# Local attention and a gated MLP on one core: all second chunks of P V get 96 rows, and the keys of each tile lie side by side

## The chip, the cores and the metric

The kernel runs on one core of a Trainium2 chip. The metric is device time in microseconds for one execution, the median of several runs. A core has TensorE (PE in the profile, with its weight loads as PEld), VectorE (DVE), ScalarE (ACT), GpSimd (POOL), SyncE (SP) and 16 DMA engines.

## What is computed

Eight batches, eight heads, 512 local and 32 global tokens, head size 64. Local queries see the keys within 32 positions and all global keys, global queries see everything. The 544 x 8 rows then pass through a two-layer MLP.

```python
s_ll = scale * np.matmul(q_l, k_l.transpose(0, 1, 3, 2))
mask = np.abs(pos[:, None] - pos[None, :]) <= window          # window = 32
s_l = np.concatenate([s_lg, np.where(mask, s_ll, -1e9)], axis=-1)
out_l = np.matmul(sm(s_l), np.concatenate([v_g, v_l], axis=2))
...
h = x @ w_in                       # 4608 x 512 by 512 x 2048
g = h * np.tanh(softplus(h))
return g @ w_out                   # 4608 x 2048 by 2048 x 512
```

## The kernel before

**Attention.** Work goes by batch `b`, head pair `hp` and tile `t` of 128 queries: 128 such units. A tile needs its own 128 keys, 32 on either side where they exist, and the 32 global ones: `WIDTH = [192, 224, 224, 192]` keys. `scores` (L714) makes the scores of two tiles and both heads: per tile and head one float32 matmul for the tile's own 128 keys and one for the remaining 64 or 96. In SBUF (`qk`) the global keys stand in the middle of every tile's 128, so both matmuls read with a stride. A float32 matmul shows in the trace as two passes, each with a weight load of its own, so the eight matmuls of a task leave 16 records. The two heads lie on partitions 0 to 63 and 64 to 127 and run side by side. Then `row_max` (DVE), `expo` (ACT), a split of P into two float16 halves, and a transpose, which a DMA does from batch 1 on, and TensorE in batch 0 (`p_cross`, L774 and L788).

`pv` (L822) makes P V for one tile: for each head three matmuls over the first chunk (the tile's own 128 keys, `vf`) and three over the second (`vc`: neighbours and global keys), 64 columns each. The second chunk has `WIDTH[t] - 128` rows: 64 for tiles 0 and 3, 96 for tiles 1 and 2:

```python
k = WIDTH[t] - 128 if c else 128
for p, vl in ((0, 0), (0, 1), (1, 0)):
    T.matmul(X[u][:, t, h, :], X[pt][:k, ...], X[vx][:k, t, vl, h * 64:(h + 1) * 64], ...)
```

The tiles of `P`, `ph` and `vc` are cleared once at the start; rows 64 to 95 of `vc` are never written for tiles 0 and 3 and stay zero. The global queries have tasks of their own (`g_scores` L860, `g_pv` L914).

**MLP.** It runs over 17 blocks of 256 tokens, in float16 halves. Blocks 0 to 5 take M1 (L958), Mish on ACT, a split into `G` on ACT and DVE, and M2 (L1200). Later blocks replace M1 by a Strassen-like scheme (L1127). M2 follows M1 by `LAG2` slots, a slot being one attention unit. The weights come as 8-byte floats. DVE rebuilds each of 32 loads of 512 KB by three bit operations (L517, L524, L526), TensorE sums squares for a scale (`ws`, L538), and the scaled weights are split with the help of TensorE (L580).

**Order.** A planner (`Plan`) gives each task a cost, a priority (its slot) and buffers, and writes the order of each engine at build time; a few numbers (`BLK2`, `LAGX`, `BOOST`, `CONV1`, ...) set the slots. On the chip each engine and each DMA queue works off its list in that order.

Of the kernel before, what the change touches and what calls it, by code (L numbers as in the profile page):

```python
# [10 lines left out]
F32 = mybir.dt.float32  # L11
# [12 lines left out]
B, H, SL, SG, D = 8, 8, 512, 32, 64  # L24
HP = H // 2
# [2 lines left out]
NF = 8  # L28
TB = 256
NBLK = B * 2 + 1  # L30
KW = 640
SCALE = 0.125
EPS = 1e-9
PSC = 4096.0
# [5 lines left out]


WIDTH = [192, 224, 224, 192]
GC = 64

ST0 = 6
GLATE = 4
# [2 lines left out]
PE, DVE, ACT, POOL, DMA = "PE", "DVE", "ACT", "POOL", "DMA"  # L49
# [253 lines left out]
def attn_mish_kernel(ctx: ExitStack, tc: tile.TileContext, qk, vm, vg, qg, w1, w2, consts_in, out, w64):  # L303
    nc = tc.nc
    V, A, T, G = nc.vector, nc.scalar, nc.tensor, nc.gpsimd
# [25 lines left out]

    rings(sb,

          ("vraw", 1, [128, HP, 4, 128], F32), ("vgraw", 2, [128, 2, 128], F32), ("qg", 2, [128, HP, 64], F32),
          ("vgf", 2, [128, 2, 2, 128], F16),

          ("nm", 6, [128, 1], F32), ("sums", 3, [128, 4, 2], F32), ("rs", 2, [128, 4, 2], F32),
# [222 lines left out]
    parted = set()  # L560
# [6 lines left out]

    def w_split(j):

        parted.add(j)  # L570
        w = j // 8
        f, c, k = W[:, j + j // 8 + 1, :], sw[:, w:w + 1], ("W", j + j // 8 + 1)
        hi, lo, d = [wslot(j), "hi"], [wslot(j), "lo"], ("dg", w)
        pl.add([(ACT, act(1024)), (DVE, dve2(1024))], 0, lambda e: scaled(e, wh(j, 0), f, c), r=[k, ["sw", w]], w=[wslot(j)])
        if j in BY_PE:
            for hf in range(2):
                rest, cols = ("rest", j, hf), slice(hf * 512, (hf + 1) * 512)

# [60 lines left out]
               r=[sv, rg], w=[g])  # L639

    def qk_load(b, hp):
        stream(DMA, dma(576), lambda: load(X["qk", b, hp], qk[b, hp]), 4608, new=[("qk", ("qk", b, hp))])

    def loc(k, j, n):

        a = k[:, SL + 160 * j:SL + 160 * j + 64]
        return bass.AP(a.tensor, a.offset, [list(a.ap[0]), [160, n], [96, 2], list(a.ap[-1])])

    def v_hi(b, hp):
        vf = ("vf", b, hp)  # L650
# [45 lines left out]
    def scores(b, hp, t):  # L696
        qk, s = ("qk", b, hp), [("s", b, hp, t // 2, h) for h in range(2)]

        def go():
            for u in (t, t + 1):  # L700
                a0, c0, k = SL + 160 * u, cols(u).start, qk
                for rest in range(2):
                    for h in range(2):
                        r = slice(h * 64, h * 64 + 64)
                        if rest:
                            n = (WIDTH[u] - 128) // 32
                            x = X[k][r, a0 - 32 if u else SL + 64:][:, :32]
                            x = bass.AP(x.tensor, x.offset, [list(x.ap[0]), [96, n], list(x.ap[-1])])
                            o = X[s[h]][:, c0 + 128:c0 + WIDTH[u]]
                        else:  # L710
                            x = X[k][r, a0:a0 + 64]
                            x = bass.AP(x.tensor, x.offset, [list(x.ap[0]), [96, 2], list(x.ap[-1])])
                            o = X[s[h]][:, c0:c0 + 128]
                        T.matmul(o, X[k][r, u * 128:(u + 1) * 128], x, start=True, stop=True)  # L714
        pl.add(PE, 920, go, r=[qk], new=[("sc", s[0]), ("sc", s[1])])

    def cols(t):

        a = WIDTH[t - 1] if t % 2 else 0
        return slice(a, a + WIDTH[t])  # L720
# [42 lines left out]
    def p_cross(b, hp, t):  # L763

        P, pt, PT = ("P", b, hp, t), ("pt", b, hp, t), ("PT", b, hp, t)

        edge = WIDTH[t] - 128

        def go():
            for c in range(2):  # L770
                rows = edge if c else 128
                for h in range(2):
                    a = h * 224 + c * 128
                    T.matmul(X[PT][:rows, (c * 2 + h) * 128:(c * 2 + h + 1) * 128], X[P][:, a:a + rows], ident, is_transpose=True,  # L774
                             start=(h == c == 0), stop=False, skip_group_check=True)
        pl.add(PE, 430, go, r=[P, "consts"], new=[("h", PT)], rows=0)

        def part(p, c, rows):
            return X[pt][:rows, p * 4 + c * 2:p * 4 + c * 2 + 2, :].rearrange("p n q -> p (n q)")

        def each(fn, w=512):
            for c in range(2):
                rows = edge if c else 128
# [28 lines left out]
    def pv(b, hp, t):  # L812
        pt, vf, vc, (g, ts) = ("pt", b, hp, t), ("vf", b, hp), ("vc", b, hp), group(b, hp, t)
        u, first = ("U", *g), t == ts[0]

        def go():
            for h in range(2):
                n = 0
                for c, vx in ((0, vf), (1, vc)):
                    k = WIDTH[t] - 128 if c else 128  # L820
                    for p, vl in ((0, 0), (0, 1), (1, 0)):
                        T.matmul(X[u][:, t, h, :], X[pt][:k, p * 4 + (c * 2 + h if b < TURNED else h * 2 + c), :],  # L822
                                 X[vx][:k, t, vl, h * 64:(h + 1) * 64], start=(n == 0), stop=(n == 5))
                        n += 1
        pl.add(PE, 360, go, r=[pt, vf, vc], w=() if first else [u], new=[("u", u)] if first else ())
# [27 lines left out]
    def g_scores(b, hp):  # L853
        q, k, g = ("qg", b), ("qk", b, hp), ("g", b, hp)

        def go():
            for c0, n in ((16, 256), (0, 16)):
                for half in range(2):
                    rhs = loc(X[k], 2 * half, 2) if c0 else X[k][:, SL + GC + 16 * half:SL + GC + 16 * half + 16]
# [64 lines left out]
    def blk_x(blk):  # L924
        return (("xh", blk // 2), ("xl", blk // 2), blk % 2 * TB) if blk < 2 * B else (("xh", "g"), ("xl", "g"), 0)

    def blk_parts(blk):
        return [[x, (hp, blk % 2)] for x in blk_x(blk)[:2] for hp in range(HP)]

    def blk_start(blk):  # L930
        c = ("c", blk)
# [299 lines left out]
    BLK2 = 33.028  # L1231
    BLK3 = 39.967
    LAGX = 19.134
    BLOCKS = [9, 17, max(25, int(BLK2)), max(33, int(BLK3))]
    PACE = 0.790
    MORE = 3.680
    S1 = [int(BLOCKS[s // NF] + PACE * (s % NF)) if s < 4 * NF else s + max(18, int(LAGX)) + (int(MORE) if s >= ST0 * NF else 0) for s in range(len(steps))]
    assert all(a <= z - (n % NF == NF - 1) for n, (a, z) in enumerate(zip(S1, S1[1:])))
    LAG2 = 4
    LATER = 18  # L1240
    BOOST = 84.202
    BOOST2 = -31.868
# [6 lines left out]

    splits = []  # L1250
    F0 = 50.843
    FSTEP = 0.607
# [140 lines left out]
    RATE1 = 0.062
    CONV2 = 2.335
    RATE2 = 0.514
    FIRST1 = 6.564
# [26 lines left out]
    for i, x in enumerate(ORDER.split()):  # L1423
        a, n = x[0], int(x[1:] or 0)
# [82 lines left out]
```

## Time and profile before

| | |
|---|---|
| time, median of 3 runs | 961.41 us (961.21 to 962.45) |
| profiled execution, its own time | 960.51 us |
| its span, first to last instruction | 958.7 us |
| mean granted TensorE clock, share of full | 0.990 |
| PE busy | 927.6 us |
| DVE busy, ACT busy | 659.1 us, 575.4 us |

The profiled execution lies 0.9 us below the median. Its time exceeds its span by 1.8 us.

### The profile page before, as it was taken

Reading aid. Unit: us, or ns where it says so; the run is one execution under the profiler, and the core shown is the slowest. Engines: PE = TensorE matmul, PEld = TensorE weight load, DVE = VectorE, ACT = ScalarE, POOL = GpSimd, SP = SyncE. Lnnn points to the kernel's source line nnn. Section 1 sums busy time; section 2 is a strip of 40 time slices with the busy share of each in tenths; the row PEclk is TensorE's granted clock in tenths of the full one; section 3 lists DMA queues with packets and bytes.
Section 4 is the critical chain, followed back from the end, with each engine's and each line's share of the span. In section 5 each row is a group of like instructions: output and inputs, shape, how many; then the busy total and the mean of one; then the engine's idle time right before and its main releaser. Section 6 shows DMA issues by size and latency. Waiting matters only on the chain.

```text
span 958.7 us, 25031 instructions
## 1 busy us (share of the span) xinstructions
PE 927.6 (97%) x10180; PEld 662.5 (69%) x10180; DVE 659.1 (69%) x1869; ACT 575.4 (60%) x1292; POOL 31.3 (3%) x56
## 2 busy tenths in 40 slices
PE   3879999999999999999999999999999999999997
PEld 2647667768776676777777777777777777677673
DVE  6998747757869998798668855786578554843231
ACT  3566867758767687677667665766566553322230
POOL 6120000000000000000000000000000000000000
PEclk9989999999999999999999999999999999999999
DMA  9973125767845756745545654565445440000000
GB/s 355 344 224 130 26 61 128 138 151 121 188 82 104 146 139 114 144 114 93 109 98 125 129 115 103 118 143 108 98 108 89 78 73 26 19 23 1 23 23 23
DMA packets 203683, 106.26 MB, mean 111 GB/s; under 512 B 179632, under 2 KB 189872, under 8 KB 202544
## 3 DMA queue, kind: packets, MB, share of 16 engines
q1 hardware_dynamic: 198816, 87.62, 43.1%
q0 software_dynamic: 3888, 14.16, 4.2%
q10 hardware_dynamic: 864, 2.88, 0.8%
q8 instruction: 80, 1.31, 0.6%
q14 instruction: 35, 0.29, 0.1%
HBM read 46.42 MB, written 8.91 MB: 58 GB/s over the span
## 4 chain that ended last, share of the span: by engine, by line
PE 93%; DMA 2%; DVE 2%; ACT 1%; POOL 1%; issue 0%; SPq 0%; DVEq 0%; ACTq 0%; POOLq 0%
PE o L1200 37%; PE h L1127 22%; PE h L958 13%; PE U L822 7%; PE s L714 7%; PE g L860 2%; PE gu L914 2%; PE rest L580 2%; DMA raw<-in_w 1%; DMA W<-in_w 1%; PE ws L538 1%; DMA gpt<-gph 1%; DVE W L524 1%; DVE W L526 1%; PE PT L774 1%; POOL vc L353 0%
## 5 line engine op out<-in xcount | busy, mean ns | idle before, releaser
L1200 PE MATMUL o<-W,G 128*128 128x512 f16 x1632 | 379.2, 379 | 0.0
L1200 PEld LDWEIGHTS <-G 128*128 128x128 f16 x1632 | 151.8, 98 | 156.9 <-issue 0.3
L1127 PEld LDWEIGHTS <-W 128*128 128x128 f16 x2640 | 152.4, 98 | 13.3
L737 ACT ACTIVATE P<-P,nm 128x192 f32<-128x192 f32 (+1 forms) x256 | 117.5, 460 | 37.6 <-DVE nm L728 34.9
L958 PE MATMUL h<-xh,W 128*128 128x256 f16 x768 | 138.6, 273 | 0.5 <-ACT EE L1004 0.5
L958 PEld LDWEIGHTS <-W 128*128 128x128 f16 x1152 | 108.6, 98 | 18.8 <-issue 1.7
L958 PE MATMUL h<-xl,W 128*128 128x256 f16 x384 | 104.6, 272 | 0.0
L728 DVE CUSTOM_DVE_ANT_0 P<-s,consts 128x192 f32<-128x192 f32 (+1 forms) x256 | 90.0, 368 | 16.2 <-PE s L714 10.1
L1127 PE MATMUL h<-xh,W 128*128 128x128 f16 x960 | 88.1, 219 | 0.0
L822 PEld LDWEIGHTS <-pt 128*128 128x128 f16 (+2 forms) x1536 | 69.0, 97 | 25.1 <-ACT pt L428 1.1
L1127 PE MATMUL h<-xl,W 128*128 128x128 f16 x480 | 82.8, 219 | 0.0
L754 DVE SCALAR_TENSOR_TENSOR ph<-P,ph 128x384 f16<-128x384 f32 (+1 forms) x112 | 63.9, 588 | 21.6 <-ACT ph L428 20.2
L714 PEld LDWEIGHTS s<-qk 64*128 64x128 f32 x1024 | 63.4, 190 | 14.9 <-issue 9.9
L714 PE MATMUL s<-qk 64*128 64x128 f32 (+2 forms) x1024 | 73.2, 283 | 0.0
L1127 PE MATMUL h<-raw,W 128*128 128x128 f16 x1056 | 68.1, 219 | 0.0
L421 ACT COPY EE<-h 128x512 f32<-128x512 f32 x44 | 25.8, 586 | 64.4 <-PE h L1127 39.8
L822 PE MATMUL U<-vc,pt 96*128 96x64 f16 (+1 forms) x768 | 60.9, 193 | 0.0
L822 PE MATMUL U<-vf,pt 128*128 128x64 f16 x720 | 57.1, 194 | 1.0 <-ACT pt L428 1.0
L428 ACT ACTIVATE ph<-P 128x384 f16<-128x384 f32 (+1 forms) x108 | 55.9, 539 | 3.5 <-DMA pt<-ph 3.0
L430 DVE TENSOR_SCALAR G<-EE,c 128x512 f16<-128x512 f32 (+1 forms) x59 | 32.7, 555 | 28.5 <-ACT EE L1004 21.1
L872 DVE TENSOR_REDUCE gmx<-g 128x1 f32<-128x272 f32 x32 | 14.1, 441 | 50.6 <-PE g L860 50.5
L428 ACT ACTIVATE ob<-o,c 128x512 f32<-128x512 f32 (+1 forms) x34 | 23.0, 675 | 42.3 <-PE o L1200 42.1
(172 smaller groups left out, 1359.3 us busy)
## 6 DMA issues: line engine op xcount, KB each, us to landing
qk<-in_qk SPq DMA_DIRECT2D x32, 576.0 KB, 4.4
W<-in_w POOLq DMA_DIRECT2D x17, 512.0 KB, 7.7
out<-ob SPq DMA_DIRECT2D x33, 256.0 KB, 2.3
vraw<-in_vm SPq DMA_DIRECT2D x8, 1024.0 KB, 5.7
raw<-in_w POOLq DMA_DIRECT2D x10, 512.0 KB, 5.0
W<-in_w ACTq DMA_DIRECT2D x5, 512.0 KB, 8.3
pt<-ph SPq DMA_TRANSPOSE x112, 3.3
vc<-vgf SPq DMA_DIRECT2D x32, 48.0 KB, 3.1
```

The costliest lines, as they stand in the source:

```text
L421: A.copy(dst, src)
L428: A.activation(out=dst, in_=src, func=AF.Copy, scale=c)
L430: V.tensor_scalar(dst, src, c, None, ALU.mult)
L580: T.matmul(X[rest], X[d], f[:, cols], start=True, stop=False)
L714: T.matmul(o, X[k][r, u * 128:(u + 1) * 128], x, start=True, stop=True)
L728: pl.add(DVE, 77 + 1.03 * w, lambda: V.tensor_tensor_reduce(out=half(P, h, w), in0=X[s][:, cols(t)], in1=mask[:, m0:m0 + w], scale=-SCALE, ...
L737: pl.add(ACT, 460, lambda: A.activation(out=half(P, h, w), in_=half(P, h, w), func=AF.Exp, bias=X[nm], scale=-1.0, accum_out=X[sums][:, t, ...
L754: pl.add(DVE, dve(n), lambda: V.scalar_tensor_tensor(p_part(X[ph], t, 1), p_src(X[P], t), PSC, p_part(X[ph], t, 0), ALU.mult, ALU.subtract ...
L822: T.matmul(X[u][:, t, h, :], X[pt][:k, p * 4 + (c * 2 + h if b < TURNED else h * 2 + c), :], X[vx][:k, t, vl, h * 64:(h + 1) * 64], start= ...
L958: T.matmul(X[h][:, f * TB:(f + 1) * TB], wh(i, wl)[:, off:off + 128], X[x][:, d, o:o + TB], start=(n == 0), stop=(n == 11))
L1127: T.matmul(X[h][:, c:c + 128], form(J + jj, wl)[:, off:off + 128], x(l, d), start=(p in (1, 2, 5) and c == 0 and n == 0), stop=(n == 5), s ...
L1200: T.matmul(X[o], gp(g, blk, i)[:, f, t * 128:(t + 1) * 128], wh(8 + i, wl)[:, f * 512:(f + 1) * 512], start=(turn == 0 and n == 0), stop=( ...
```

## The change

The host lays the keys of each tile side by side: own 128, neighbours and global keys, 832 columns per head pair in place of 640, so one matmul per tile and head makes all its scores. In P V and in the TensorE transposes of batch 0 the second chunk always has 96 rows; for tiles 0 and 3 the last 32 of them meet rows of `vc` that hold zeros. `vgraw` goes from two buffers to one. The planner's numbers differ. The rest of the diff (assertions) issues nothing.

```diff
-KW = 640
+OWN = [0, 192, 416, 640]
+KW = 832
...
-GC = 64
+GC = 128
...
-          ("vraw", 1, [128, HP, 4, 128], F32), ("vgraw", 2, [128, 2, 128], F32), ("qg", 2, [128, HP, 64], F32),
+          ("vraw", 1, [128, HP, 4, 128], F32), ("vgraw", 1, [128, 2, 128], F32), ("qg", 2, [128, HP, 64], F32),
...
-        stream(DMA, dma(576), lambda: load(X["qk", b, hp], qk[b, hp]), 4608, new=[("qk", ("qk", b, hp))])
+        stream(DMA, dma(672), lambda: load(X["qk", b, hp], qk[b, hp]), 5376, new=[("qk", ("qk", b, hp))])
...
-                a0, c0, k = SL + 160 * u, cols(u).start, qk
-                for rest in range(2):
-                    for h in range(2):
-                        r = slice(h * 64, h * 64 + 64)
-                        if rest:
-                            n = (WIDTH[u] - 128) // 32
-                            x = X[k][r, a0 - 32 if u else SL + 64:][:, :32]
-                            x = bass.AP(x.tensor, x.offset, [list(x.ap[0]), [96, n], list(x.ap[-1])])
-                            o = X[s[h]][:, c0 + 128:c0 + WIDTH[u]]
-                        else:
-                            x = X[k][r, a0:a0 + 64]
-                            x = bass.AP(x.tensor, x.offset, [list(x.ap[0]), [96, 2], list(x.ap[-1])])
-                            o = X[s[h]][:, c0:c0 + 128]
-                        T.matmul(o, X[k][r, u * 128:(u + 1) * 128], x, start=True, stop=True)
+                for h in range(2):
+                    r = slice(h * 64, h * 64 + 64)
+                    T.matmul(X[s[h]][:, cols(u)], X[qk][r, u * 128:(u + 1) * 128], X[qk][r, SL + OWN[u]:SL + OWN[u] + WIDTH[u]],
+                             start=True, stop=True)
...
-                rows = edge if c else 128
+                rows = 96 if c else 128
...
-                    k = WIDTH[t] - 128 if c else 128
+                    k = 96 if c else 128
...
-    LAGX = 19.134
+    LAGX = 19.303
...
-    LAG2 = 4
-    LATER = 18
-    BOOST = 84.202
+    LAG2 = 3
+    LATER = 17
+    BOOST = 107.966
...
-    CONV1 = 2.438
+    CONV1 = 1.970
...
-    AHEAD_DMA = 11.576
+    AHEAD_DMA = 5.257
```

**TensorE, a score task** (batch 5, head pair 3, tiles 2 and 3; `s_<hp>_<half>_<head>`). Before:

```order
L714 MATMUL s_3_1_0_8419<-qk_104 128x128
L714 MATMUL s_3_1_1_8420<-qk_104 128x128
L714 MATMUL s_3_1_0_8419<-qk_104 128x96
L714 MATMUL s_3_1_1_8420<-qk_104 128x96
L714 MATMUL s_3_1_0_8419<-qk_104 128x128
L714 MATMUL s_3_1_1_8420<-qk_104 128x128
L714 MATMUL s_3_1_0_8419<-qk_104 128x64
L714 MATMUL s_3_1_1_8420<-qk_104 128x64
```

The same task of the change, on the same engine:

```order
L705 MATMUL s_3_1_0_8217<-qk_104 128x224
L705 MATMUL s_3_1_1_8218<-qk_104 128x224
L705 MATMUL s_3_1_0_8217<-qk_104 128x192
L705 MATMUL s_3_1_1_8218<-qk_104 128x192
L1121 LDWEIGHTS W
```

Eight matmuls become four, of the same 416 columns per head. The rows of a P V task read alike in both, since the order does not print the rows of its operands.

**TensorE, ahead of the first M1 matmul** (`h_0`; `rest` splits a weight tile, `ws` sums squares, `gu`, `g` and `s` are attention). Before:

```order
L581 MATMUL rest_0_883<-W,minus 128x512
L914 LDWEIGHTS vgg_93
L914 MATMUL gu_0_891<-gpt_0_843,vgg_93 128x64
...
L860 MATMUL g_1_914<-qk_104,qg_125 64x16 x2
...
L581 MATMUL rest_1_929<-W,minus 128x512
L714 MATMUL s_2_1_0_936<-qk_105 128x128
...
L714 MATMUL s_2_1_1_937<-qk_105 128x64
L958 LDWEIGHTS W
L958 MATMUL h_0_953<-xh_446,W 128x256
```

With the change:

```order
L583 MATMUL rest_0_821<-W,minus 128x512
L582 MATMUL rest_1_827<-W,dg_637 128x512
L583 LDWEIGHTS minus
L583 MATMUL rest_1_827<-W,minus 128x512
L539 LDWEIGHTS W
L539 MATMUL ws_612<-W 128x128
...
L952 LDWEIGHTS W
L952 MATMUL h_0_843<-xh_423,W 128x256
```

The tasks `gu_0`, `g_1` and `s_2_1` moved from ahead of the first M1 matmul to behind it.

**DVE, ahead of the first weight scale** (L545, L546 after; operations on `raw` are those of the second matrix's weights). Before:

```order
L524 SCALAR_TENSOR_TENSOR W<-raw_107,W 128x512
L832 TENSOR_TENSOR x_1_0_555<-U_1_0_496,rs_1_0_357 128x256
L526 SCALAR_TENSOR_TENSOR W<-W 128x2x256
L526 SCALAR_TENSOR_TENSOR W<-raw_107,W 128x512
L517 TENSOR_SCALAR W<-W 128x2x256
L517 TENSOR_SCALAR W<-raw_108 128x512
L524 SCALAR_TENSOR_TENSOR W<-W 128x2x256
L524 SCALAR_TENSOR_TENSOR W<-raw_108,W 128x512
L526 SCALAR_TENSOR_TENSOR W<-W 128x2x256
L526 SCALAR_TENSOR_TENSOR W<-raw_108,W 128x512
L517 TENSOR_SCALAR W<-W 128x512
L545 ISA wd_623,wm_622<-ws_212,consts 128x128
```

With the change:

```order
L518 TENSOR_SCALAR W<-raw_107 128x512
L527 SCALAR_TENSOR_TENSOR W<-W 128x2x256
L822 RECIPROCAL rs_2_0_540<-rs_2_0_540 128x4
L525 SCALAR_TENSOR_TENSOR W<-raw_107,W 128x512
L518 TENSOR_SCALAR W<-W 128x512
L546 ISA wd_586,wm_585<-ws_213,consts 128x128
```

Four operations on `raw` that stood ahead of the scale now stand behind it: one L517, one L524 and two L526.

## Rows read from the trace of the kernel before

**Rows 1.** The page: span, busy time by engine, the chain that ended last by engine.

```profile
span 958.7 us, 25031 instructions
...
PE 927.6 (97%) x10180; PEld 662.5 (69%) x10180; DVE 659.1 (69%) x1869; ACT 575.4 (60%) x1292; POOL 31.3 (3%) x56
...
PE 93%; DMA 2%; DVE 2%; ACT 1%; POOL 1%; issue 0%; SPq 0%; DVEq 0%; ACTq 0%; POOLq 0%
```

**Rows 2.** Busy time in six stretches; columns: stretch, us, each engine's busy time, clock, DMA.

```profile
0.00:50.00 50.00, 30.32 (x273) 20.75 (x274) 40.14 (x113) 23.36 (x74) 20.66 (x37) 0.93 0.94 346
50.00:76.00 26.00, 20.99 (x165) 12.44 (x166) 24.59 (x80) 15.55 (x45) 6.30 (x11) 0.80 0.75 234
76.00:300.00 224.00, 222.50 (x2172) 159.42 (x2173) 156.07 (x510) 164.05 (x372) 1.93 (x5) 1.00 0.53 111
300.00:425.00 125.00, 125.00 (x1256) 88.92 (x1255) 109.49 (x309) 91.14 (x200) 0.78 (x1) 1.00 0.61 121
425.00:800.00 375.00, 375.00 (x4736) 275.86 (x4735) 267.09 (x765) 238.47 (x536) 1.62 (x3) 1.00 0.53 106
800.00:958.00 158.00, 153.75 (x1593) 105.14 (x1589) 61.71 (x96) 42.80 (x68) 0.00 (x0) 1.00 0.06 20
```

**Rows 3.** The timeline of PE, a P V task with 96 rows.

```profile
565.12 0.25 PE L822 MATMUL U<-vf,pt 128*128 128x64 f16 x3
565.21 0.25 PE L822 MATMUL U<-vc,pt 96*128 96x64 f16 x3
...
565.47 0.22 PE L1127 MATMUL h<-xh,W 128*128 128x128 f16 x1
```

**Rows 4.** The timeline of PE, a score task and a P V task with 64 rows.

```profile
571.36 1.11 PE L714 MATMUL s<-qk 64*128 64x128 f32 x16
572.40 0.26 PE L822 MATMUL U<-vf,pt 128*128 128x64 f16 x3
572.60 0.26 PE L822 MATMUL U<-vc,pt 64*128 64x64 f16 x3
...
573.17 0.23 PE L1127 MATMUL h<-xh,W 128*128 128x128 f16 x1
```

**Rows 5.** Groups of matmuls by line and shape, busy us and mean ns.

```profile
L714 PE MATMUL s<-qk 64*128 64x128 f32 x512 | 60.2, 311 | 0.0
...
L822 PE MATMUL U<-vc,pt 64*128 64x64 f16 x384 | 33.0, 193 | 0.0
```

**Rows 6.** The timeline of PE's weight loads within that score task, pieces of it.

```profile
571.36 0.19 PEld L714 LDWEIGHTS s<-qk 64*128 64x128 f32 x2
...
571.47 0.30 PEld L714 LDWEIGHTS s<-qk 64*128 64x128 f32 x4
...
572.14 0.20 PEld L714 LDWEIGHTS s<-qk 64*128 64x128 f32 x2
```

**Rows 7.** The timeline of PE, wide float32 matmuls (two passes of 512 columns).

```profile
121.64 1.02 PE L580 MATMUL rest<-W,dg 128*128 128x512 f32 x2
122.50 0.38 PE L581 MATMUL rest<-W,minus 128*128 128x512 f16 x1
```

**Rows 8.** The timeline of PE before the first M1 matmul.

```profile
71.54 0.25 PE L914 MATMUL gu<-gpt,vgg 128*128 128x64 f16 x3 [1.80 <-DMA gpt<-gph]
...
76.89 0.28 PE L958 MATMUL h<-xh,W 128*128 128x256 f16 x1
```

**Rows 9.** The timeline of DVE, two of the weights' bit operations.

```profile
47.12 0.68 DVE L524 SCALAR_TENSOR_TENSOR W<-raw,W 128x512 int32<-128x512 int32 x1
47.72 0.69 DVE L526 SCALAR_TENSOR_TENSOR W<-W 128x512 int32<-128x512 int32 x1
```

**Rows 10.** The page's DMA issues and groups: the loads of qk, M1's weight loads, G.

```profile
L958 PEld LDWEIGHTS <-W 128*128 128x128 f16 x1152 | 108.6, 98 | 18.8 <-issue 1.7
...
L430 DVE TENSOR_SCALAR G<-EE,c 128x512 f16<-128x512 f32 (+1 forms) x59 | 32.7, 555 | 28.5 <-ACT EE L1004 21.1
...
qk<-in_qk SPq DMA_DIRECT2D x32, 576.0 KB, 4.4
```

More of the change, by code (lines that the diff above doesn't have):

```diff
@@ L568, in w_split @@
     def w_split(j):
+        assert j % 8 == 0 or j - 1 in parted
         parted.add(j)
@@ L641, in qk_load, with loc @@
     def qk_load(b, hp):
-        stream(DMA, dma(576), lambda: load(X["qk", b, hp], qk[b, hp]), 4608, new=[("qk", ("qk", b, hp))])
-    def loc(k, j, n):
-        a = k[:, SL + 160 * j:SL + 160 * j + 64]
-        return bass.AP(a.tensor, a.offset, [list(a.ap[0]), [160, n], [96, 2], list(a.ap[-1])])
+        stream(DMA, dma(672), lambda: load(X["qk", b, hp], qk[b, hp]), 5376, new=[("qk", ("qk", b, hp))])
+    def loc(k, j):
+        a = k[:, SL + OWN[j]:SL + OWN[j] + 128]
+        return bass.AP(a.tensor, a.offset, [list(a.ap[0]), [OWN[j + 1] - OWN[j], 2], list(a.ap[-1])])
     def v_hi(b, hp):
@@ L765, in p_cross @@
         P, pt, PT = ("P", b, hp, t), ("pt", b, hp, t), ("PT", b, hp, t)
-        edge = WIDTH[t] - 128
         def go():
             for c in range(2):
-                rows = edge if c else 128
+                rows = 96 if c else 128
                 for h in range(2):
@@ L782, in each @@
             for c in range(2):
-                rows = edge if c else 128
+                rows = 96 if c else 128
                 fn(c, rows, X[PT][:rows, c * 256:c * 256 + 256])
@@ L858, in go @@
                 for half in range(2):
-                    rhs = loc(X[k], 2 * half, 2) if c0 else X[k][:, SL + GC + 16 * half:SL + GC + 16 * half + 16]
+                    rhs = loc(X[k], 2 * half) if c0 else X[k][:, SL + GC + 16 * half:SL + GC + 16 * half + 16]
                     T.matmul(X[g][half * 64:half * 64 + 64, c0:c0 + n], X[q][:, hp, :], rhs, start=True, stop=True)
@@ L927, in blk_parts @@
     def blk_parts(blk):
-        return [[x, (hp, blk % 2)] for x in blk_x(blk)[:2] for hp in range(HP)]
+        need = [[x, (hp, blk % 2)] for x in blk_x(blk)[:2] for hp in range(HP)]
+        for x, part in need if blk < 2 * B else ():
+            assert x in pl.place and pl.state[pl.place[x]].get(part, (None,))[0] is not None, ("early", x, part)
+        return need
     def blk_start(blk):
@@ L1229, in attn_mish_kernel @@
     steps = [(blk, i if blk < ST0 else (4, 5, 0, 1, 6, 7, 2, 3)[n]) for blk in range(NBLK) for n, i in enumerate(range(NF))]
-    BLK2 = 33.028
+    BLK2 = 33.020
     BLK3 = 39.967
-    LAGX = 19.134
+    LAGX = 19.303
     BLOCKS = [9, 17, max(25, int(BLK2)), max(33, int(BLK3))]
     PACE = 0.790
-    MORE = 3.680
+    MORE = 3.414
     S1 = [int(BLOCKS[s // NF] + PACE * (s % NF)) if s < 4 * NF else s + max(18, int(LAGX)) + (int(MORE) if s >= ST0 * NF else 0) for s in range(len(steps))]
     assert all(a <= z - (n % NF == NF - 1) for n, (a, z) in enumerate(zip(S1, S1[1:])))
-    LAG2 = 4
-    LATER = 18
-    BOOST = 84.202
-    BOOST2 = -31.868
+    LAG2 = 3
+    LATER = 17
+    BOOST = 107.966
+    BOOST2 = -30.333
     def at(u):
@@ L1251, in attn_mish_kernel @@
     F0 = 50.843
-    FSTEP = 0.607
+    FSTEP = 0.564
     SFREE = S1[3 * NF + 4]
@@ L1389, in attn_mish_kernel @@
     ORDER = "k0 m w0 b w1 w2 k1 w3 w4 k2 k3 g"
-    LOAD1 = -10.338
-    LOADS1 = -0.019
-    CONV1 = 2.438
[L1393 to L1396, printed above, removed]
+    LOAD1 = -14.947
+    LOADS1 = -0.118
+    CONV1 = 1.970
+    RATE1 = 0.082
+    CONV2 = 3.153
+    RATE2 = 0.276
+    FIRST1 = 6.958
     STEP1 = 1.000
-    FIRST2 = 6.491
-    STEP2 = 0.001
-    AHEAD_DMA = 11.576
+    FIRST2 = 6.280
+    STEP2 = 0.010
+    AHEAD_DMA = 5.257
     def weights():
@@ L1465 @@
     qt = pairs(q_l.reshape(B, HP, 2, SL, D))
-    lb = k_l.reshape(B, H, 16, 32, D)
-    gb = k_g.reshape(B, H, 1, 32, D)
-    blocks = [x for t in range(4) for x in (lb[:, :, 4 * t:4 * t + 2], gb, lb[:, :, 4 * t + 2:4 * t + 4])]
-    kt = pairs(np.concatenate(blocks, axis=2).reshape(B, HP, 2, KW, D))
+    lb = np.concatenate([k_l.reshape(B, H, 16, 32, D), k_g.reshape(B, H, 1, 32, D)], axis=2)
+    blocks = [x for t in range(4) for x in [*range(4 * t, 4 * t + 4), *[4 * t - 1] * (t > 0), 16, *[4 * t + 4] * (t < 3)]]
+    kt = pairs(lb[:, :, blocks].reshape(B, HP, 2, KW, D))
     qk = np.concatenate([qt, kt], axis=3)
```

## The prediction

> **What bounds the kernel now.** I read the page first. PE is busy for 97% of the span, and the chain that ended last is 93% PE [rows 1]. A share is an average, so I took busy time by stretches next [rows 2]. Up to 50 us the DMA engines are 94% busy and PE 61%. From 50 to 76 us DVE is busy 24.6 of 26 us, PE 21.0, and the granted clock is 0.80. From 76 us on PE has 1.5 us of idle time up to 300 us, none up to 800, and 4.25 at the end, where the last rows are stored. So whatever shortens PE's list behind 76 us shortens the kernel by as much, as long as nothing else then comes late. What the list loses ahead of 76 us is worth less, since DMA and DVE set the pace there.
>
> Then I looked at single tasks on PE's timeline, by the start of one line to the start of the next, because durations of pipelined matmuls overlap.
>
> **P V.** A task whose second chunk has 96 rows takes from 565.12 to 565.47, 0.35 us for twelve matmuls. Three go in 0.09 us, and the step from 128 to 96 rows costs nothing that can be seen [rows 3]. A task with 64 rows takes from 572.40 to 573.17, 0.77 us, and its first three matmuls, of the same 64 columns, take 0.20 us until the 64-row ones start [rows 4]. Each change between 128 and 64 rows therefore costs some 0.10 us, and such a task has four: 0.40 us, nearly the whole difference of 0.42. With 96 rows all four go. The columns stay, and so does the number of instructions.
>
> There are 384 matmuls of 64 rows, six to a task, so 64 tasks [rows 5]. Four of them run ahead of 76 us (tiles 0 of batch 0). That leaves 60, at 0.40 us: 24.0 us. In the order of before some 12 of them are followed by a score task or a global one, which also leaves the full array. The last change stays there, in front of another task: 12 x 0.10 = 1.2 us less. P V gives **22.8 us**. The bounds are 18 us (three changes of 0.10 in each of 60) and 25 us (0.42 in each).
>
> **Scores.** A score task takes 1.04 us [rows 4]. Its 16 records are 8 pairs, both heads side by side. The weight loads of the pairs start 0.11 us apart, from 571.36 over 571.47 to 572.14, seven steps in 0.78 us, whatever the width of the piece (128, 96 or 64 columns) [rows 6]. So the weight loads set the pace, and narrow pieces wait for theirs. The change has 4 pairs of 224 or 192 columns. How fast a wide pass streams I take from the float32 matmuls of 512 columns: two passes from 121.64 to 122.50, 0.86 us for 1024 columns, 0.84 ns each [rows 7]. Four passes over 2 x (224 + 192) = 832 columns take 0.70 us, and their later loads, 0.11 us each, hide under passes of at least 0.16 us. The first load of 0.11 us stays in the open. So does the way out: the last load starts at 572.14, takes 0.11, its piece of 64 columns 0.05, and the next task starts at 572.40, which is 0.10 later. That makes 0.11 + 0.70 + 0.10 = 0.91 us, 0.13 less than now. No row shows such a task, so I take 0.12. The task has 512 records of 128 columns, eight to a task, so 64 tasks [rows 5], 57 of them behind 76 us: **6.8 us**. The bounds are 0 (the merged matmul brings nothing) and 57 x 0.24 = 13.7 us (the first load hides too).
>
> **Transposes of batch 0.** Four tasks behind 76 us have two changes less, at 0.10 us: **0.8 us**. The copies on ACT and DVE keep their columns and cost the same.
>
> **The start.** Here the order moves, and I can only bound it. The first M1 matmul starts at 76.89, and ahead of it stands `gu_0`, which waited 1.80 us for a transposing DMA [rows 8]. With the change `gu_0`, `g_1` and `s_2_1` come behind the first M1 matmuls, which wait for no such transfer. On DVE four operations of the second matrix move behind the first weight scale, three at 0.60 us [rows 9] and a shorter one, so the scale comes some 2 us earlier. Against this the four `qk` loads of batch 0 grow by 4 x 96 KB, which at 346 GB/s [rows 2] is 1.1 us more of DMA in a stretch that DMA fills. The gain cannot pass PE's 5.0 us of idle time between 50 and 76 us. The loss could be 1.1 us plus about 2 us if the `ws` passes, now strewn singly among other work, each wait for DVE. I take the stall that goes, about **2 us** of gain, between -3 and +5.
>
> **What costs nothing, and its cover.** 28 more `qk` loads are 96 KB larger. One of 576 KB lands in 4.4 us [rows 10], so one of 672 KB takes an estimated 5.1 us. It is issued about three slots ahead of its scores, a slot being some 6 us (128 units in some 760 us), and DMA is 53 to 61% busy there [rows 2]. Without that cover 28 x 0.7 us = 20 us would show. The single `vgraw` buffer makes a load wait for the split of the batch before. In SP's order it stands right next to the small `vc` and `vgg` moves that need the same split, so nothing new queues behind it, and VectorE reads the data of batch 1 only after the first weight scale.
>
> **New waits.** `LAG2` falls from 4 to 3: M2 follows M1 more closely, and with a shorter PE list DVE has less time for the same work. From 300 to 425 us DVE is busy 109.5 of 125 us [rows 2]. At 6 us a unit some 21 P V tasks lie there, half of them of 64 rows, and 10 score tasks, so PE's list gets 10 x 0.40 + 10 x 0.12 = 5.2 us shorter and DVE's share goes from 88% to 91%. Average room is left, but not everywhere: I allow **1.5 us** of new stalls, between 0 and 4.
>
> **The sum**, against the profiled execution's 960.5 us: 960.5 - 22.8 - 6.8 - 0.8 - 2 + 1.5 = 929.6 us. The median of the runs lies 0.9 us above that execution, so I predict 930.5 us.
>
> **Rivals.**
> 1. DVE becomes the bound where it is busiest. It speaks for this that 88% is high, that the Strassen sums lie there and that the order is fixed. It speaks against it that PE had not one stall there. If PE loses all that it gains from 76 to 425 us (350 of the 724 us in which attention runs behind 76 us, so about 14 us of 30), the time is 944 us; half of it gives 937.
> 2. The merged scores stream no faster: the 0.11 us between weight loads is then not what paces them. The sum lacks 6.8 us: 937 us. The even steps under uneven pieces speak against it.
> 3. A pair of 64-row matmuls could share the array, and with 96 rows this is lost. The twelve matmuls would be worth less at 64 rows: six at half of 0.03 us, 0.09 us per task, 5.4 us in 60: 936 us. The rows show no such half: with the changes taken off, 64-row matmuls go at the pace of the others [rows 3, 4]. The Trainium skill, TensorEngine Tiling (Array Packing), section Theoretical Speedup, gives a factor of up to 2 for a contraction of at most 64 rows, which speaks against padding to 96; the trace does not bear it out here, as all these matmuls start at the same partition.
> 4. Slower than before: M2 waits for `G` in every step of blocks 0 to 5, because it follows a slot earlier. There are 1152 M1 matmuls, 24 to a step [rows 10], so 48 steps; the gain of 30.9 us is gone at 0.64 us of wait per step. At 1 us the time is 979 us. Against it: three slots are about 18 us, and what lies between M1 and M2 is Mish and a split, three operations of some 0.6 us like the one at 555 ns [rows 10].
> 5. The start gains its full 5 us, and the first score load hides: 921 us.
>
> **How the numbers follow.** The forecast, 924 to 936 us with new stalls of a few us, gets 0.73. Rival 1 gets 0.10, rivals 2 and 3 together 0.08, rival 4 0.03, rival 5 0.06. The range of 922 to 941 us holds the forecast, rivals 2 and 3, and most of rival 1 and of rival 5. A difference of 0.2% is about what a measurement of this kernel can tell from no change. Only rival 4, or rival 1 far beyond its price, reaches that line: faster 0.96, same 0.01, slower 0.03.
>
> **What would show it.** P V tasks of tiles 0 and 3 at 0.35 us with three matmuls in 0.09; score tasks at 0.91 us with eight records; P V's four changes gone from PE's timeline; the first M1 matmul near 70 us; PE without idle time from there on. The prediction is wrong if PE shows idle time of more than 5 us behind 76 us, with DVE or ACT as the releaser, if score tasks stay near 1.04 us, or if the start loses what the steady part gains.

## The result and the profile after

The changed kernel takes **926.36 us** (median of 4 runs, 925.18 to 927.0); the kernel before took 961.31 in the runs beside it (958.92 to 962.45). The ratio is 0.9638, 95% interval 0.9617 to 0.9659. The profiled execution took 926.49 us, span 924.7. The forecast was 930.5.

From the page of the changed kernel (busy time by engine, the chain by engine, the `qk` loads), beside [rows 1, 10]:

```profile
span 924.7 us, 23984 instructions
...
PE 890.7 (96%) x9668; PEld 628.7 (68%) x9668; DVE 655.0 (71%) x1866; ACT 588.8 (64%) x1305; POOL 32.5 (4%) x56
...
PE 84%; DVE 9%; DMA 3%; ACT 2%; POOL 1%; issue 1%; SPq 0%; DVEq 0%; ACTq 0%; POOLq 0%
...
qk<-in_qk SPq DMA_DIRECT2D x32, 672.0 KB, 5.2
```

PE's busy time falls by 36.9 us (927.6 to 890.7) and the span by 34.0, so PE's time without work (span less busy) grows from 31.1 to 34.0 us. DVE (655.0 us of work) and ACT (588.8) have about as much to do as before (659.1 and 575.4). The share of the chain that is not PE grows from 7% to 16%: the other engines have come closer.

Busy time by stretches of the changed kernel, as in [rows 2]:

```profile
0.00:50.00 50.00, 28.33 (x248) 19.11 (x248) 40.11 (x117) 23.94 (x77) 21.88 (x38) 0.97 0.96 349
50.00:76.00 26.00, 22.47 (x208) 15.79 (x210) 25.67 (x75) 19.98 (x47) 5.14 (x9) 1.00 0.78 239
76.00:300.00 224.00, 220.27 (x2078) 152.79 (x2075) 166.31 (x543) 172.01 (x390) 2.60 (x5) 0.99 0.57 121
300.00:425.00 125.00, 124.89 (x1270) 87.89 (x1268) 109.44 (x325) 96.21 (x214) 1.50 (x2) 1.00 0.67 138
425.00:800.00 375.00, 375.00 (x4661) 271.85 (x4659) 269.94 (x747) 245.21 (x532) 1.33 (x2) 1.00 0.51 104
```

Between 76 and 800 us PE has 3.73 + 0.11 = 3.8 us of idle time; it had 1.5. Up to 50 us its idle time grows from 19.7 to 21.7 us. From 50 to 76 us it falls from 5.0 to 3.5, and the granted clock there is 1.00, the full 2.4 GHz, in place of 0.80.

The timeline of PE in the changed kernel, a score task and the P V task behind it, answers to [rows 3, 4]:

```profile
573.34 0.97 PE L705 MATMUL s<-qk 64*128 64x224 f32 x8
574.24 0.26 PE L813 MATMUL U<-vf,pt 128*128 128x64 f16 x3
574.34 0.25 PE L813 MATMUL U<-vc,pt 96*128 96x64 f16 x3
574.43 0.25 PE L813 MATMUL U<-vf,pt 128*128 128x64 f16 x3
574.52 0.25 PE L813 MATMUL U<-vc,pt 96*128 96x64 f16 x3
574.61 0.22 PE L1121 MATMUL h<-xh,W 128*128 128x128 f16 x1
```

The score task takes 0.90 us (it took 1.04), the P V task 0.37 (with 64 rows it took 0.77), three matmuls in 0.09 to 0.10. The groups by line and shape, beside [rows 5]:

```profile
L813 PE MATMUL U<-vc,pt 96*128 96x64 f16 x768 | 55.8, 192 | 0.0
...
L705 PE MATMUL s<-qk 64*128 64x224 f32 x256 | 39.3, 382 | 0.0
```

No P V matmul has 64 rows any more. The timeline of the start, beside [rows 8]: the first M1 matmul runs at 66.32 in place of 76.89, `gu` stands behind it and still waits for its transposing DMA, and M2 begins at 96.12, where it began at 100.49:

```profile
66.32 0.27 PE L952 MATMUL h<-xh,W 128*128 128x256 f16 x1
...
73.77 0.25 PE L905 MATMUL gu<-gpt,vgg 128*128 128x64 f16 x3 [0.93 <-DMA gpt<-gph]
...
96.12 1.24 PE L1194 MATMUL o<-W,G 128*128 128x512 f16 x5
```

PE has the same attention, M1 and weight tasks ahead of the first M2 matmul in both kernels, so the start has gained 100.49 - 96.12 = 4.4 us. The other 34.0 - 4.4 = 29.6 us came behind it.

Up to that matmul PE was busy for 75.3 us before and is for 69.3 now, while its idle time grows from 25.2 to 26.8 us. So the start gains by shorter work, not by shorter waits. Not all of that comes from the change of shapes. The `rest` matmuls are the same twenty and ten in both kernels, and take 18.0 us before and 15.6 now, since the granted clock differs. One of three `rest` pairs of the kernel before that ran at the lower level (1.2 GHz; the granted clock from 53 to 58 us is 0.50) took twice the 1.02 us of [rows 7]:

```profile
54.10 2.02 PE L580 MATMUL rest<-W,dg 128*128 128x512 f32 x2
```

In the changed kernel one pair, at 88.01 us, ran so. Why the clock was granted differently is not shown; each kernel has one profiled execution.

What PE waited for, in the view of the waits (us in total, times, longest):

```profile
PE VT L662 <- ACT dv L429: 15.5, 1, 15.5
PE ws L539 <- DVE W L527: 5.0, 6, 2.5
...
PE U L813 <- DMA pt<-ph: 1.8, 2, 1.2
PE gu L905 <- DMA gpt<-gph: 1.2, 2, 0.9
```

The first of them is PE's wait at the very start, which was 14.8 us before. M2 is not in the list.

### The profile page after: what moved, and what is told of

The parts are those of the page before. It is cut to its first block, busy times and chain, and to the rows that moved or that the text cites. A ratio compares the mean times of both kernels' runs of the same rounds, so it can differ in the third digit from the quotient of the medians.

```text
span 924.7 us, 23984 instructions
## 1 busy us (share of the span) xinstructions
PE 890.7 (96%) x9668; PEld 628.7 (68%) x9668; DVE 655.0 (71%) x1866; ACT 588.8 (64%) x1305; POOL 32.5 (4%) x56
## 4 chain that ended last, share of the span: by engine, by line
PE 84%; DVE 9%; DMA 3%; ACT 2%; POOL 1%; issue 1%; SPq 0%; DVEq 0%; ACTq 0%; POOLq 0%
PE o L1194 35%; PE h L1121 23%; PE h L952 11%; PE s L705 5%; PE U L813 4%; PE g L851 2%; PE gu L905 2%; DVE W L525 1%; DVE qk L1037 1%; DVE W L527 1%; DVE P L720 1%; DMA W<-in_w 1%; DMA pt<-ph 1%; DVE W L518 1%; PE rest L582 1%
## 5 line engine op out<-in xcount | busy, mean ns | idle before, releaser
L813 PEld LDWEIGHTS <-pt 128*128 128x128 f16 (+1 forms) x1536 | 59.2, 97 | 19.7 <-issue 7.1
L705 PE MATMUL s<-qk 64*128 64x192 f32 (+1 forms) x512 | 64.2, 369 | 0.0
L813 PE MATMUL U<-vc,pt 96*128 96x64 f16 x768 | 55.8, 192 | 0.0
L813 PE MATMUL U<-vf,pt 128*128 128x64 f16 x720 | 52.3, 193 | 2.6 <-DMA pt<-ph 1.8
L705 PEld LDWEIGHTS s<-qk 64*128 64x128 f32 x512 | 43.1, 190 | 16.1 <-issue 7.7
L729 ACT ACTIVATION_READ_ACCUMULATOR P<-P,nm 128x1 f32 x256 | 48.1, 188 | 0.0
L1147 DVE TENSOR_TENSOR VX<-h,VX 128x512 f32<-128x512 f32 x22 | 15.1, 687 | 43.0 <-ACT VX L422 43.0
```

The costliest lines, as they stand in the source:

```text
L705: T.matmul(X[s[h]][:, cols(u)], X[qk][r, u * 128:(u + 1) * 128], X[qk][r, SL + OWN[u]:SL + OWN[u] + WIDTH[u]], start=True, stop=True)
L729: pl.add(ACT, 460, lambda: A.activation(out=half(P, h, w), in_=half(P, h, w), func=AF.Exp, bias=X[nm], scale=-1.0, accum_out=X[sums][:, t, ...
```

## Experiments

Twelve kernels ran. Four take a part of the change back, eight separate the planner's numbers and the order from the shapes. "Old" numbers are those of the kernel before. The kernel before had medians of 960.36 to 961.68 us beside them; each ratio is against the one beside it. At the end of this section a table has them all.

### The rows of P V

**e1_pv64** gives tiles 0 and 3 their 64 rows back in P V; order and numbers stay.

```diff
-                    k = 96 if c else 128
+                    k = WIDTH[t] - 128 if c else 128
```

> The changed kernel, but the second chunk of P V has 64 rows again in tiles 0 and 3; the order is that of the change. My theory, a price of about 0.10 us for each change between 128 and 64 rows: four come back in each of 64 tasks, 60 of them where PE sets the pace, so about 23 us more than the change (949 us), and P V tasks of those tiles at 0.76 us. Rival, the gain came from the new order and numbers of the planner: less than 5 us more (under 932 us).

It took 949.22 us (948.33 to 950.06), ratio 0.9888 [0.9871, 0.9904]: 22.9 us more than the changed kernel, where the term was 22.8. A task of tile 3 on its timeline:

```profile
589.00 0.26 PE L813 MATMUL U<-vf,pt 128*128 128x64 f16 x3
589.19 0.26 PE L813 MATMUL U<-vc,pt 64*128 64x64 f16 x3
589.38 0.26 PE L813 MATMUL U<-vf,pt 128*128 128x64 f16 x3
589.58 0.26 PE L813 MATMUL U<-vc,pt 64*128 64x64 f16 x3
589.77 0.23 PE L1121 MATMUL h<-xh,W 128*128 128x128 f16 x1
```

Every group of three, of 128 rows or of 64, takes 0.19 to 0.20 us in place of 0.09. The price is paid at each change, in both directions.

**e2_pv68** uses 68 rows there, four more than 64.

```diff
-                    k = 96 if c else 128
+                    k = (68 if t in (0, 3) else 96) if c else 128
```

> The changed kernel, but the second chunk of tiles 0 and 3 has 68 rows in place of 96. My theory, what counts is whether the matmul leaves the full array, and 68 rows do not: as the change within 1 us, 0.35 us a task. Rival, the price grows as the rows fall short of the first chunk's 128: 68 rows cost nearly what 64 cost, some 20 us more (946 us).

926.5 us (926.03 to 928.84), ratio 0.9653 [0.9636, 0.967], as the changed kernel. On its timeline a task with 68 rows:

```profile
574.26 0.26 PE L813 MATMUL U<-vf,pt 128*128 128x64 f16 x3
574.36 0.25 PE L813 MATMUL U<-vc,pt 68*128 68x64 f16 x3
574.45 0.25 PE L813 MATMUL U<-vf,pt 128*128 128x64 f16 x3
```

With 68 rows three matmuls take 0.09 us again. It isn't a difference of rows that costs (128 to 68, or 128 to 96), but the step from 128 down to 64.

**e3_pv64_grouped** keeps the 64 rows and all twelve matmuls, but runs the first chunks of both heads before the second ones: two changes of rows per task in place of four.

```diff
-            for h in range(2):
-                n = 0
-                for c, vx in ((0, vf), (1, vc)):
-                    k = 96 if c else 128
-                    for p, vl in ((0, 0), (0, 1), (1, 0)):
+            for c, vx in ((0, vf), (1, vc)):
+                k = WIDTH[t] - 128 if c else 128
+                for h in range(2):
+                    for n, (p, vl) in enumerate(((0, 0), (0, 1), (1, 0))):
...
```

> The changed kernel with 64 rows again in tiles 0 and 3, but within a task both heads' first chunks come first and both heads' second chunks after them, so the rows change twice and not four times; the matmuls are the same. My theory, a price per change: half of what four changes cost, 11 to 12 us more than the change (938 us), tasks at 0.56 us. Rival, each 64-row matmul is itself slower, 0.40 us over six of them: as with four changes, 23 us more (949 us).

936.47 us (936.2 to 937.95), ratio 0.9755 [0.9741, 0.977]: 10.1 us more than the changed kernel. Its timeline:

```profile
581.29 0.35 PE L812 MATMUL U<-vf,pt 128*128 128x64 f16 x6
581.57 0.34 PE L812 MATMUL U<-vc,pt 64*128 64x64 f16 x6
581.85 0.23 PE L1120 MATMUL h<-xh,W 128*128 128x128 f16 x1
```

The task takes 0.56 us: 0.36 for twelve matmuls and 0.10 for each of two changes. So the price belongs to the change and not to the 64-row matmul, six of which go in 0.28 - 0.10 = 0.18 us, as six of 128 rows do. The Trainium skill, TensorEngine Tiling (Array Packing), section Key Properties, says that "Changing tiling mode (not just tile) drains the TensorE". These three runs agree in that each change between 128 and 64 rows has a price, 0.10 us, which the page does not give; that a drain is what costs it no trace shows.

### The scores

**e4_scores_split** keeps the new layout and order but cuts each score matmul into 128 columns and the rest.

```diff
-                for h in range(2):
-                    r = slice(h * 64, h * 64 + 64)
-                    T.matmul(X[s[h]][:, cols(u)], ..., X[qk][r, SL + OWN[u]:SL + OWN[u] + WIDTH[u]], ...)
+                for z in (slice(0, 128), slice(128, WIDTH[u])):
+                    for h in range(2):
+                        r = slice(h * 64, h * 64 + 64)
+                        T.matmul(X[s[h]][:, cols(u)][:, z], ..., X[qk][r, SL + OWN[u]:SL + OWN[u] + WIDTH[u]][:, z], ...)
```

> The changed kernel, but each score matmul is again two, 128 columns and the rest, of keys side by side. My theory, the weight loads 0.11 us apart pace the narrow pieces: 0.13 us more in each of 57 tasks, 7 to 8 us more than the change (934 us), tasks at 1.04 us. Rival, it was the strided read of the keys that was slow and not the number of loads: as the change within 1 us, tasks near 0.91 us.

937.27 us (935.13 to 937.7), ratio 0.9756 [0.974, 0.9772]: 10.9 us more, not 7 or 8. The task is back at 1.04 us, with keys that lie side by side, so the stride played no part, and the number of pieces did:

```profile
581.83 1.11 PE L706 MATMUL s<-qk 64*128 64x128 f32 x16
582.87 0.26 PE L814 MATMUL U<-vf,pt 128*128 128x64 f16 x3
```

64 tasks at 0.14 us are 9.0 us, seven of them in the start, which I had left out; PE's busy time is 9.4 us longer. The other 1.3 us of the span are idle time, to which I can put no single cause. That the weight loads pace the narrow pieces is read from their even steps of 0.11 us under pieces of 128, 96 and 64 columns. In the changed kernel's task the loads of the pairs start at 573.34, 573.44, 573.63 and 573.82 us: behind the first, the steps are 0.19 us, what 224 columns take at 0.84 ns each. M2 begins at 98.2 us in this run and at 98.3 in e1_pv64, where it begins at 96.12 in the changed kernel: undoing either part gives back 2 us of the start.

### The parts alone, in the order of before

**f1_before_96** is the kernel before with 96 rows in P V and in the transposes. Order and numbers are those of before.

```diff
-                rows = edge if c else 128
+                rows = 96 if c else 128
...
-                    k = WIDTH[t] - 128 if c else 128
+                    k = 96 if c else 128
```

> The kernel before with 96 rows in every second chunk of P V and of the transposes of batch 0, and nothing else: key layout, score matmuls, numbers and order are those of before. My theory, 0.40 us in each task of tiles 0 and 3 behind 76 us: 22.8 + 0.8 us less than before, 937 us. Rival, part of that gain needs the new order: less than 18 us, over 942 us.

940.7 us (938.35 to 943.27), ratio 0.9793 [0.976, 0.9827]. By the medians the gain is 19.8 us (960.46 less 940.7), between the 23.6 of the theory and the 18 of the rival. In the profiled execution, which took 942.9 us, PE's busy time falls by 27.3 us, the span by 17.7: 9.6 us come back as idle time. So waits take a part of the gain in this order. Two that have grown (the first from 4.1 us; the second is not in the list of the kernel before):

```profile
PE ws L538 <- DVE W L526: 6.0, 8, 1.3
...
PE U L820 <- DMA pt<-ph: 3.0, 3, 1.8
```

**f4_before_newnums** is the kernel before with the numbers of the change and nothing else.

```diff
-    LAG2 = 4
+    LAG2 = 3
...
-    AHEAD_DMA = 11.576
+    AHEAD_DMA = 5.257
```

> The kernel before with all the planner's numbers of the change; matmuls and key layout are those of before. My theory, the start gains some 2 to 3 us and the rest stays: 958 us. Rival, the new numbers fit only the shorter tasks: 961 us or more, with waits of PE behind the start.

964.95 us (963.72 to 965.43), ratio 1.0041 [1.0028, 1.0054]. By themselves the numbers are worth nothing here; they cost 4.5 us. The theory missed and the rival held: from 76 to 300 us PE is idle for 7.1 us, where it was for 1.5.

### The numbers of the planner

**f2_after_oldnums** is the changed kernel with all old numbers (`LAG2 = 4`, `AHEAD_DMA = 11.576` and the sixteen others).

> The changed kernel with all the planner's numbers of the kernel before. My theory, the start gains because three attention tasks move behind the first M1 matmul, which the numbers decide: about 3 us more than the change (929 us), first M2 matmul near 99 us, less waiting of P V than with the new numbers. Rival, the start gains because score tasks and P V are shorter there too: as the change within 1 us.

954.73 us (952.56 to 956.22), ratio 0.9937 [0.9913, 0.9961]: **28 us** more than the changed kernel, where I had expected 3. Its matmuls are those of the changed kernel, task for task, but its idle time is 54.8 us (span 952.9 less 898.1 busy) against 34.0. The waits grow:

```profile
PE ws L539 <- DVE W L527: 9.7, 9, 2.5
PE U L813 <- DMA pt<-ph: 8.5, 8, 3.5
PE gu L905 <- DMA gpt<-gph: 5.1, 6, 1.6
```

The longest stands at 188.50 us. The chain there (start, duration, what):

```profile
180.28 0.95 PE s L705 x8
...
182.28 0.48 ACT ph L429
...
182.78 0.64 DVE ph L746
...
183.47 4.99 DMA pt<-ph
...
188.50 0.82 PE U L813 x12
```

From the scores of a tile to its P V is one chain of 8.2 us, 5.0 of them the transposing DMA, and this order leaves less than that between them. The timeline of SP's queue shows the transposes issued one behind the other at this place:

```profile
182.06 1.20 SPq L599 DMA_TRANSPOSE xl<-xs  x1
183.47 1.23 SPq L599 DMA_TRANSPOSE pt<-ph  x1
184.75 1.31 SPq L599 DMA_TRANSPOSE gpt<-gph  x1
```

The stretch in windows (PE, PEld, DVE, ACT, POOL, clock, DMA share, GB/s):

```profile
180.00:190.00 10.00, 4.96 (x69) 3.59 (x68) 5.00 (x19) 5.36 (x16) 0.00 (x0) 0.84 1.00 182
190.00:200.00 10.00, 10.00 (x82) 7.88 (x80) 6.62 (x20) 7.88 (x13) 0.00 (x0) 0.82 0.59 142
```

Here the stall is paid for twice. PE stands still for 5 us of the first ten, 3.5 of them in one piece up to 188.50. The granted clock falls while PE stands still (0.71 from 186 to 188 us), is at its lower level, 1.2 GHz, when PE goes on (0.50 from 188 to 192, 0.59 from 192 to 194), and at the full 2.4 GHz from 194 on, with PE busy throughout: 0.82 is the mean of the two. At the lower level the twelve matmuls of the P V task behind the stall take 0.63 us (188.50 to 189.13) in place of 0.37. PE's whole busy time, for the same matmuls, is 898.1 in place of 890.7 us, at a mean granted clock of 0.988 in place of 0.995.

**f3_after_oldstart** takes back only the numbers of the weights' path (`LOAD1` to `AHEAD_DMA`), **g3_after_oldsteady** only the other eight (`BLK2`, `LAGX`, `MORE`, `LAG2`, `LATER`, `BOOST`, `BOOST2`, `FSTEP`).

> The changed kernel with only those numbers of before that set the weights' path (loads, bit operations, splits); the slots of M1, M2 and the attention are those of the change. My theory: the start loses what it loses with all the old numbers, first M2 matmul near 99 us, and the rest is as in the change: 929 us. Rival, the slots matter for the start and these numbers do not: first M2 matmul near 96 us, 926 us.

> The changed kernel with the slots of attention, M1 and M2 as before (BLK2, LAGX, MORE, LAG2, LATER, BOOST, BOOST2, FSTEP) and the numbers of the weights' path as in the change; the complement of the run of 949 us. If the weights' path is what costs, this one stays near 926 to 932 us. If any mixture of the two sets fits no order, it loses 15 us or more: 941 us and up. I lean to the first, 931 us, since in the run with all old numbers the idle time lay ahead of 200 us.

948.53 us (946.56 to 949.76), ratio 0.9872 [0.9846, 0.9898], and 940.45 us (939.91 to 945.22), ratio 0.9796 [0.9771, 0.9821]: 22 and 14 us more than the changed kernel. The first missed both its theory and its rival, and the second came out near 941, against which I had leant. Neither half of the numbers is the one that matters; each half costs when it alone is put back, and the two losses overlap (22 + 14 is more than 28). In the second of them PE stands at the same kind of place as above:

```profile
180.10 0.26 PE L813 MATMUL U<-VX,pt 128*128 128x64 f16 x3 [2.61 <-DMA pt<-ph]
```

### Why the old numbers fit no more

With the same old numbers, the kernel before with 96 rows takes 941 us and the changed kernel 955. Between them lie the merged scores, the wider loads, the single `vgraw` buffer, other strides in the key reads of the global scores, and two entries in which the planner notes the duration and size of a `qk` load.

**g1_oldnums_oldcost** is the changed kernel with old numbers and with these entries as before; the loads stay wide.

```diff
-        stream(DMA, dma(672), lambda: load(X["qk", b, hp], qk[b, hp]), 5376, new=[("qk", ("qk", b, hp))])
+        stream(DMA, dma(576), lambda: load(X["qk", b, hp], qk[b, hp]), 4608, new=[("qk", ("qk", b, hp))])
```

> The changed kernel with the planner's numbers of before (the run that took 955 us), and now also the planner's two entries for a qk load, its assumed duration and size, as before (576 columns and 4608 bytes in place of 672 and 5376). The loads themselves stay wide, the scores merged, the vgraw buffer single. On PE this is nearly the order of before with merged scores. Theory: the 28 us went into the new order that the two entries bring about, since the old numbers were fitted to another one: about 941 (before with 96 rows) less 7.3 for the scores, 934 us, with 936 allowed. Rival: the wider loads or the single buffer themselves come late: 950 us or more.

**h1_before_96_vg1** is the kernel before with 96 rows and one `vgraw` buffer.

```diff
-          ... ("vgraw", 2, [128, 2, 128], F32), ...
+          ... ("vgraw", 1, [128, 2, 128], F32), ...
```

> The kernel before with 96 rows in P V and in the transposes (the run of 941 us), and with one buffer for vgraw in place of two; keys, scores and numbers as before, the order on PE nearly so. Theory: the single buffer costs nothing: 941 us, within 2. Rival: it holds up SP's queue, so the load of v comes late and PE waits for the transposes: 948 us or more.

**h2_before_96_vg1_cost** is the same with the two entries raised (`dma(672)`, 5376), though its loads stay narrow.

> As the run before (96 rows, one vgraw buffer), with the planner's two entries for a qk load raised to 672 columns and 5376 bytes, though the loads stay at 576. No transfer and no matmul changes its size; only the order does (some 3000 rows on PE differ). Theory, the order is at fault: 953 to 960 us, that is 941 plus 12 to 20. Rival, the entries matter only through the real loads: 941 us, within 3.

They took 939.92 us (937.45 to 943.83), ratio 0.9783 [0.9753, 0.9813]; 940.22 us (938.27 to 943.29), ratio 0.9785 [0.976, 0.9811]; and 954.77 us (953.32 to 955.17), ratio 0.9929 [0.9912, 0.9945].

- The single buffer costs nothing (940.2 against 940.7).
- The two entries cost 14.6 us without any transfer or matmul that changes (954.77 - 940.22), and 14.8 in the changed kernel (954.73 - 939.92). That is the order alone: some 3,000 of PE's rows stand elsewhere. In the profiled executions of h1 and h2 PE's idle time grows by 7.3 us and its busy time, for the same matmuls, by 5.8, with a granted clock of 0.98 in place of 1.00 from 76 to 300 us. The waits for `pt` go from 1.5 us to 5.9. The line for `pt` in the view of PE's waits, without the raised entries and with them:

```profile
PE U L820 <- DMA pt<-ph: 1.5, 3, 0.8
```

```profile
PE U L820 <- DMA pt<-ph: 5.9, 6, 2.4
```

- Merging the scores (with the wider loads) brings nothing in the order of the old entries: 939.92 against 940.22 (g1, h1), though each task takes 0.13 us less. It brings nothing in the order of the raised entries either: 954.73 against 954.77 (f2, h2), where PE's busy time falls by 8.9 us and its idle time grows by 8.5. In both pairs PE has the same tasks in the same order. In the first, PE's busy time falls by 6.5 us (901.2 to 894.7), and its idle time grows by 6.2. Of this 2.9 us are already lost when M2 begins, at 104.76 in place of 101.83, and the waits of `gu` for `gpt` go from 2.9 to 6.6 us; the wider loads in the first 76 us fit that, but no run has them by themselves. I had expected 934; this was a miss on the scores, and right on the entries.

All runs; idle is the span less PE's busy time, in the profiled execution, which for f1, g1, h1 and g3 took 1.8 to 4.8 us more than the median beside it (945.22 us for g3):

| | time, us | span | PE busy | idle |
|---|---|---|---|---|
| before | 961.31 | 958.7 | 927.6 | 31.1 |
| changed | 926.36 | 924.7 | 890.7 | 34.0 |
| e1 64 rows | 949.22 | 946.4 | 911.5 | 34.9 |
| e2 68 rows | 926.5 | 924.7 | 889.6 | 35.1 |
| e3 64 rows, two changes | 936.47 | 935.1 | 899.5 | 35.6 |
| e4 scores split | 937.27 | 935.4 | 900.1 | 35.3 |
| f1 before, 96 rows | 940.7 | 941.0 | 900.3 | 40.7 |
| f4 before, new numbers | 964.95 | 962.8 | 925.3 | 37.5 |
| f2 changed, old numbers | 954.73 | 952.9 | 898.1 | 54.8 |
| f3 changed, old weights' path | 948.53 | 947.9 | 898.2 | 49.7 |
| g3 changed, other numbers old | 940.45 | 943.1 | 896.4 | 46.7 |
| g1 changed, old numbers and entries | 939.92 | 939.9 | 894.7 | 45.2 |
| h1 as f1, one buffer | 940.22 | 940.2 | 901.2 | 39.0 |
| h2 as h1, new entries | 954.77 | 953.3 | 907.0 | 46.3 |

Read down the last two columns: the first four experiments change PE's busy time and leave the idle time at 35 us; all kernels that have the new shapes, whole or in part, with old numbers, all or half of them, have 5 to 21 us more of it than the changed kernel.

## Why the prediction was right

**P V, -22.8.** Right in mechanism and size: putting the 64 rows back costs 22.9 us, the four changes 0.10 us each (e1, e3). Of the 22.9 some 2 lie ahead of the first M2 matmul (98.3 against 96.12 us in e1), where five of the 64 tasks stand, four of them not counted in the term. So the term as such was about 2 us too high. Its deduction for tasks in front of a score or global task is borne out: in the changed kernel P V tasks in front of those take 0.45 us, the others 0.36.

**Scores, -6.8.** Right for the task: 0.90 us where 0.91 was worked out, which fits that the weight loads set the pace of narrow pieces, and that the first load does not hide. 57 tasks at 0.14 are 8.0; taking the merge back costs 10.9 in all, with the seven tasks of the start and some waits. That is their worth in the order of the change; in both orders with the old numbers the merge brought nothing (g1 against h1, f2 against h2).

**Transposes, -0.8.** Not tried by themselves.

**The start, -2.** Undersized: by the first M2 matmul the start had gained 4.4 us. I counted the shorter tasks only behind 76 us, since DMA and DVE set the pace ahead of it; but undoing either P V's rows or the merged scores gives back 2 us there (e1, e4), so in the order of the change they tell in the start too. In the order of before they don't: with 96 rows alone M2 begins at 101.54 us, 1.1 later than before (f1). Of the step that I had named, `gu` no longer in front of M1, half is seen: that wait of `gu` is 0.93 us where it was 1.80. The stall was not what went: PE's idle time ahead of M2 grew by 1.7 us. The granted clock, which the sum left out, took part with the 2.4 us of `rest`. No run separates it from what the new order gave.

**New stalls, +1.5.** The number fits: the idle time from 76 to 800 us grew by 2.3 us. The reason given does not carry it, so this term came out right by luck. I argued that DVE's average room (88 to 91% from 300 to 425 us) leaves the stalls small. DVE indeed did not become the bound there: PE was idle for 0.11 us of those 125. But kernels with the same tasks lost 11 to 21 us more than this one to idle time (g1, f2), mostly elsewhere: 8 and 18 us of it lie ahead of 300 us. PE waited there above all in `ws`, for the weights that DVE rebuilds (9.4 and 9.7 us in all), and in P V and `gu` for transposing DMAs (10.3 and 13.6). What kept the stalls at 2 us is the order that the new numbers give with the changed shapes and entries; why this order fits is not shown. I had passed over the numbers, apart from `LAG2` and the start, as if the order would stay as tight by itself. With the old numbers the same sum would have missed by about 24 us (954.73 against 930.5).

**The qk loads** land in 5.2 us, as estimated (5.1), and in the steady part they are hidden.

**Rivals.** DVE as the bound: not seen. Scores no faster: refuted by the task's 0.90 us, although with the old numbers it would have come true in the total (g1, f2), for another reason: PE's idle time grows by what the tasks save. Pairs of 64-row matmuls that share the array, as the Trainium skill's factor of 2 has it (TensorEngine Tiling (Array Packing), section Theoretical Speedup): no sign of it here; six take 0.18 us at 64 rows as at 128 (e3). M2 waiting for `G`: M2 is not among PE's waits. The start's full 5 us: nearly, 4.4. The 2.4 us over the forecast 2 are the larger part of the 4 us by which the time lies under the forecast.

What stays open: which of the eighteen numbers does it. The two halves are not additive, and no single number was varied. Nor is it shown why merging the scores pays in the order of the change alone.

## What to carry to other kernels

Count the changes of rows between full and half array in a stream of small matmuls, not only the columns: at 0.10 us each they cost as much here as the three matmuls between them. Padding the rows takes the changes away, and grouping the matmuls halves their number. A saving on the bounding engine shows only as far as the order keeps the others ahead; where a planner's costs and numbers set the order, a shorter task needs them found anew, and their worth can't be read from the numbers or from average busy shares. Here 28 of the 35 us are lost when the old numbers stay with the changed shapes and entries (f2), and 13.6 when the planner's entries stay old as well (g1). To see it, run the new shapes with the old numbers and the old shapes with the new ones, and compare span less busy time.

## What the runs showed of the hardware that was not expected

- The step lies between 64 and 68 rows: with 68 a matmul goes at the pace of 96 or 128, with 64 the stream pays 0.10 us at every change. A change from 96 rows to a matmul of 128 rows that fills 64 columns (`g`) has the same price: in the changed kernel a P V task in front of `g` takes 0.45 us (all ten behind 110 us, the one up to 299.01 us for example), one in front of M1 or M2 0.36.
- A transposing DMA takes SP 1.2 us to issue and 5.0 us to land in a stretch where the DMA engines' busy share was 1.00 (f2; its median is 3.2 us in the changed kernel); there it is the longest link between the scores of a tile and its P V.
- A stall of PE can cost more than its length: in f2 the granted clock was at 1.2 GHz when PE went on at 188.50 us, and until some 193.5 us its matmuls took longer (a P V task 0.63 us in place of 0.37).
